# Token weights transposed by DMA between gated loads, column-tile transposes for q and k, and half of a batch prepared one stage later

## The chip, the cores and the metric

The kernel runs on one core of one Trainium2 chip. The metric is the device time of one execution in microseconds (us), as a median of several runs; lower is better. A profiled execution also gives a trace: when each instruction began and ended, what it waited for, when each DMA landed, and the share of the TensorE clock that was granted. The span in a trace (first to last instruction) is about 2 us shorter than the device time (in the profiled run of the kernel before 172.6 us against 174.73). PE is TensorE, DVE is VectorE, ACT is ScalarE, POOL is GpSimd, SP is SyncE. In this kernel GpSimd does almost nothing but issue the loads, which change fp32 to bf16 on the way (the "software queue", q0 in the profile). SyncE issues the transposes by DMA and the stores (the "hardware queue", q1).

## The reference, cut to what matters

```python
def _attn_ref(q, k, v, n_global, n_local):      # q, k, v: (4, 8, 768, 64)
    scores = scale * np.matmul(q, k.transpose(0, 1, 3, 2))
    # a window of 96 tokens, 8 global tokens, a bias that falls with the distance
    ...
    a = np.exp(scores - np.max(scores, axis=-1, keepdims=True))
    a = a / (np.sum(a, axis=-1, keepdims=True) + 1e-09)
    return np.matmul(a, v)

def _moe_ref(x, w_theta, w_tok_r, w_tok_i, w_ch):   # x: (4, 768, 512)
    theta = x @ w_theta
    zr, zi = x * np.cos(theta), x * np.sin(theta)
    y = np.einsum('ts,bsd->btd', w_tok_r, zr) + np.einsum('ts,bsd->btd', w_tok_i, zi)
    u = x + y
    return u + np.maximum(u @ w_ch, 0.0)
```

Attention gives x; then three stages follow for each batch: theta, the mixing over tokens with the two 768x768 token weights, and the channel product. The kernel overlaps the mixing of batch b with the attention of batch b+1. "The first mixing" is the stage in which batch 0 is mixed and batch 1's attention is computed.

## The kernel before

The loads are issued at the start, in one order, by GpSimd. The token weights come in by rows and are transposed, because the mixing as it is written takes them as its stationary operand (lhsT) with the source token on the partitions. PE transposes them into PSUM and DVE copies them out:

```python
def load_w():
    nc.gpsimd.dma_start(out=w_theta_bf, in_=...)
    for tt in range(0, NT, 2):
        for wi, src in enumerate((moe_w_tok_r, moe_w_tok_i)):
            w2 = moe.tile([T, 2, S], BF, name="w_nat", bufs=6)
            nc.gpsimd.dma_start(out=w2, in_=src[tt * T:(tt + 2) * T, :].rearrange(...))
            w_nat[wi, tt], w_nat[wi, tt + 1] = w2[:, 0], w2[:, 1]
    nc.gpsimd.dma_start(out=w_ch_bf, in_=...)

def trans_w(tt, copy=nc.vector.tensor_copy):
    for wi in range(2):
        ps = ps_small([T, NT, T], BF)
        for st in range(NT):
            nc.tensor.transpose(ps[:, st, :], w_nat[wi, tt][:, st * T:(st + 1) * T], ident)
        (copy if wi else nc.vector.tensor_copy)(out=w_tokT[wi][:, :, tt * T:(tt + 1) * T], in_=ps)
...
load_w()
load_all_qk(1)      # batch 1's q and k
load_all_v(1)       # batch 1's v
load_all_qk(2)
```

For batches 1 and 2, q and k of a pair of heads are put side by side by DVE (qkn), transposed by PE, and copied out by DVE (qT) and ACT (kT):

```python
def prep_copy(b, p):
    ...
    for i_ in range(2):
        nc.vector.tensor_copy(out=qkn[:, :, i_].rearrange("p t h d -> p h t d"),
                              in_=qk[:, i_, 2 * p:2 * p + 2])
def prep(b, p):
    ...
    for i_, dst in ((0, qT), (1, kT)):
        for t_ in range(NT):
            nc.tensor.transpose(ps[:, t_, :], qkn[:, t_, i_].rearrange("p h d -> p (h d)"), ident)
        # then qT copied by DVE, kT by ACT, and kG (DVE) made from kT
```

DVE makes a copy of batch 1's v (vG) before nearly all of batch 1's score products in its instruction order. And x of batches 1 to 3 is transposed by DMA (xT) before theta:

```python
def xtrans(b, p, ...):
    anchor["sp"] = nc.sync.dma_start_transpose(out=xT_sb[b][:, p, :]..., in_=x_sb[b][:, p]...)
```

The softmax here doesn't subtract the row's maximum and nothing guards it: scores larger than these inputs give would overflow.

Of the kernel before, what the change touches and what calls it, by code (L numbers as in the profile page):

```python
# [10 lines left out]
BF = mybir.dt.bfloat16  # L11
# [5 lines left out]
def kernel(  # L17
# [13 lines left out]
    nc = tc.nc  # L31
    B, H, S, D = q.shape
    T = 128
# [22 lines left out]
    def ps_small(shape, dtype):  # L56
        return small.tile(shape, dtype, name="ps", tag="ps")
# [90 lines left out]

    w_theta_bf = const.tile([T, NC, DM], BF)
    w_ch_bf = const.tile([T, NC, DM], BF)  # L150
    w_nat = {}
    w_tokT = [const.tile([T, NT, S], BF, name=f"w_tokT_{wi}") for wi in range(2)]

    def load_w():
        nc.gpsimd.dma_start(out=w_theta_bf, in_=moe_w_theta.rearrange("(c p) n -> p c n", p=T))
        for tt in range(0, NT, 2):
            for wi, src in enumerate((moe_w_tok_r, moe_w_tok_i)):
                w2 = moe.tile([T, 2, S], BF, name="w_nat", bufs=6)
                nc.gpsimd.dma_start(
                    out=w2, in_=src[tt * T:(tt + 2) * T, :].rearrange("(a p) s -> p a s", p=T))  # L160
                w_nat[wi, tt], w_nat[wi, tt + 1] = w2[:, 0], w2[:, 1]
        nc.gpsimd.dma_start(out=w_ch_bf, in_=moe_w_ch.rearrange("(c p) n -> p c n", p=T))

    def trans_w(tt, copy=nc.vector.tensor_copy):
        for wi in range(2):
            ps = ps_small([T, NT, T], BF)
            for st in range(NT):
                nc.tensor.transpose(ps[:, st, :], w_nat[wi, tt][:, st * T:(st + 1) * T], ident)
            (copy if wi else nc.vector.tensor_copy)(out=w_tokT[wi][:, :, tt * T:(tt + 1) * T], in_=ps)


    def warm(n):
        ps = ps_small([T, 512], FP)
# [13 lines left out]
    def behind(eng):  # L187

        return tc.issue_after(anchor[eng]) if eng in anchor else nullcontext()
# [29 lines left out]
                out=kG, in_=kT[:, T:(NT - 1) * T].rearrange("p (t n) -> p t n", t=NT - 2))  # L219
            nc.vector.tensor_copy(out=kG[:, :, 0:NG], in_=kT[:, None, 0:NG].to_broadcast([T, NT - 2, NG]))  # L220

    qkns = {}

    def prep_copy(b, p):
        qk = loads[b][0]
        qkn = qkns[b, p] = att.tile([T, NT, 2, 2, D], BF, name="qkn", bufs=2)
        with behind("dve"):
            for i_ in range(2):
                nc.vector.tensor_copy(  # L229
                    out=qkn[:, :, i_].rearrange("p t h d -> p h t d"), in_=qk[:, i_, 2 * p:2 * p + 2])  # L230

    def prep(b, p):
        if p == 0:
            prep_copy(b, 0)
        if p + 1 < NP:
            prep_copy(b, p + 1)
        qkn = qkns[b, p]
        qT = att.tile([T, S], BF, name="qT", bufs=6)
        kT = att.tile([T, S], BF, name="kT", bufs=6)
        for i_, dst in ((0, qT), (1, kT)):  # L240
            ps = ps_small([T, NT, T], BF)
            with behind("pe"):
                for t_ in range(NT):
                    nc.tensor.transpose(ps[:, t_, :], qkn[:, t_, i_].rearrange("p h d -> p (h d)"), ident)  # L244

            dst = dst.rearrange("p (n t) -> p n t", t=NT)
            src = ps.rearrange("p t n -> p n t")
            if i_ == 0:
                nc.vector.tensor_copy(out=dst, in_=src)
            else:  # L250
                nc.scalar.copy(out=dst, in_=src)

        qkT[(b, p)] = [qT, kT, None]
        kglob(b, p)

    def prep_dma(b, p):
        qk = loads[b][0]
        qkT[(b, p)] = [None, None, None]
        for i_ in (1, 0):
            to = qkT[(b, p)][i_] = att.tile([T, S], BF, name=("qT", "kT")[i_], bufs=6)  # L260
            with behind("sp"):
                nc.sync.dma_start_transpose(
                    out=to.rearrange("p (t s) -> p t s", t=NT),
                    in_=qk[:, i_, 2 * p:2 * p + 2].rearrange("p h t d -> p (h t d)"))
# [138 lines left out]
    def mix(b, tt, g):  # L403
        if g == 0:
            pss["mix"] = ps_small([T, DM], FP)
        ps = pss["mix"]
        for st in (2 * g, 2 * g + 1):
            for wi in range(2):
                anchor["pe"] = nc.tensor.matmul(  # L409
                    ps, lhsT=w_tokT[wi][:, st, tt * T:(tt + 1) * T], rhs=zri[b][:, wi, st, :],  # L410
                    start=(st == 0 and wi == 0), stop=(st == NT - 1 and wi == 1)).ins
        if g == NT // 2 - 1:
            u_sb[b, tt] = moe.tile([T, DM], BF, name="u", bufs=6)
            anchor["dve"] = nc.vector.tensor_add(  # L414
                u_sb[b, tt].rearrange("p (g d) -> p g d", g=NP), x_sb[b][:, :, tt, :],
                ps.rearrange("p (g d) -> p g d", g=NP)).ins
# [28 lines left out]
    def load_all_qk(b):  # L445
        alloc_qk(b)
        load_qk(b, 0, 8)

    def load_all_v(b):
        alloc_v(b)  # L450
        load_v(b, 0, 8)


    gate = const.tile([1, 1], BF)

    def load_behind(b, tile):
        g = nc.gpsimd.tensor_copy(out=gate, in_=tile).ins
        with tc.issue_after(g):
# [3 lines left out]
    def attention_steps(b, preps):  # L462

        steps = []
        add = lambda w, f, *a: steps.append((w, lambda: f(*a)))
        add(0, alloc_x, b)
        chunks = [(p, c) for p in range(NP) for c in range(NT // 2)]
        ahead = [preps[:1], preps[1:2], preps[2:]] if preps else [[]] * 3
        if b == B - 1:
            add(0, kglob, b, 0)  # L470
        for i_ in range(0, len(chunks), 2):
            steps.append((1800, lambda i_=i_: [scores(b, *pc) for pc in chunks[i_:i_ + 2]]))
            if i_ == 0:
                add(0, vglob, b, 0, H)
            if b == B - 1 and i_ in (0, 2, 6):
                add(0, kglob, b, (1, 2, 0, 3)[i_ // 2])
            if i_ == 8:
                steps.extend((1536, f) for f in ahead[0])
            for p in [p for p in range(NP) if (i_ // 2, p) in ((2, 0), (3, 1), (5, 2))]:
                add(1600, lambda p=p: [values(b, p, 0), values(b, p, 1)])  # L480
                add(800, xtrans, b, p)
        steps.extend((1536, f) for f in ahead[1])
        add(1600, lambda: [values(b, NP - 1, 0), values(b, NP - 1, 1)])
        add(800, xtrans, b, NP - 1)
        steps.extend((1536, f) for f in ahead[2])
        return steps
# [14 lines left out]
            side[i_][1]()  # L501
            i_ += 1

    load_w()
    load_all_qk(1)
    load_all_v(1)
    load_all_qk(2)
    alloc_x(0)
# [56 lines left out]
            xtrans(0, p - 1, act if p == NP - 1 else dve)  # L565
    values(0, NP - 1, 0)
    values(0, NP - 1, 1)
    trans_w(0, nc.scalar.copy)
    xtrans(0, NP - 1)
    for c in range(NT // 2):  # L570
        theta(0, c, 0)
# [8 lines left out]
    for b in range(B):  # L580
        nxt = b + 1 if b + 1 < B else None
        lag = 3
        th = [lambda c=c, j=j: theta(b, c, j) for c in range(NT // 2) for j in range(2)]
        pre = [lambda p=p: prep(1, p) for p in range(NP)] if b == 0 else []
        ahead = [[lambda p=p: prep(2, p) for p in range(NP)], [lambda p=p: prep_dma(3, p) for p in range(1)],
                 [], []][b]
        order = th[:4] + rest[:2] + th[4:] + rest[2:] if b else []
        if b == 2:
            order[:0] = [lambda p=p: prep_dma(3, p) for p in range(1, NP)]
        if b == 1:  # L590
            order.insert(0, lambda: load_behind(3, xT_sb[1][0:1, NC - 1, 0:1]))
        for f in order:
            f()
        main = []
        for tt in range(NT):
            for g in range(NT // 2):
                if (b, tt) != (B - 1, NT - 1):
                    main.append((2048, lambda tt=tt, g=g: mix(b, tt, g)))
                if b == 0 and g == 1 and tt + 1 < NT:
                    main.append((1536, lambda tt=tt: trans_w(tt + 1)))  # L600
                if tt >= lag and g == 0 and (b, tt) != (B - 1, NT - 1):
                    main.append((2048, lambda tt=tt: chan(b, tt - lag)))
                if b == 0 and tt and g == 1:
                    main.append((512, lambda tt=tt: utrans(b, tt - 1)))
            if b and (b, tt) != (B - 1, NT - 1):
                main.append((0, lambda tt=tt: utrans(b, tt)))
        side = [(1536, f) for f in pre]
        if b == 0:
            side[:0] = [(0, lambda: load_all_v(2))]
            side.append((0, lambda: (alloc_qk(3), load_qk_tokens(3, 0, H // 2))))  # L610
        side += attention_steps(nxt, ahead) if nxt else []
        weave(main, side, 0.3 if b == 0 else 0.0, 0.9)
        rest = [lambda tt=tt, b=b: chan(b, tt) for tt in range(NT - lag, NT)]
        if b == 0:
            rest.insert(1, lambda b=b: utrans(b, NT - 1))
# [44 lines left out]
```

## Time and profile before

| | before |
|---|---|
| median of 3 runs | 175.32 us (175.06 to 175.37) |
| span in the profile | 172.6 us |
| PE, DVE, ACT busy | 159.9, 128.5, 99.1 us |
| mean granted clock | 0.996 |

The page of the profile: first the busy time of each engine, then the span in 40 slices of 4.3 us, each digit the busy share of a slice in tenths.

```profile
PE 159.9 (93%) x1482; PEld 83.5 (48%) x1482; DVE 128.5 (74%) x288; ACT 99.1 (57%) x124; POOL 37.9 (22%) x45
...
PE   6479979999999999999999998999999989999991
...
DVE  7678965678999999999587588597786837724443
...
PEclk9999999999999999999999999999999999999998
DMA  5999999999999999879999997787138571323335
```

PE looks full from the seventh slice on. The row DMA is full too, from the second slice to the sixteenth: the loads run without a gap for 65 us. Windows of 5 us say the same in numbers. The last column is what the DMA moved in GB/s, counted in the bf16 that it writes; the DMA share before it is not used here:

```profile
core 0: us, PE busy (x) PEld busy (x) DVE busy (x) ACT busy (x) POOL busy (x), PEclk, DMA share, GB/s
20.00:25.00 5.00, 4.16 (x64) 2.17 (x62) 4.22 (x12) 3.26 (x4) 2.44 (x3) 1.00 1.16 209
30.00:35.00 5.00, 5.00 (x24) 2.18 (x23) 3.38 (x9) 5.00 (x7) 0.00 (x0) 1.00 1.28 205
...
45.00:50.00 5.00, 4.83 (x61) 3.18 (x59) 5.00 (x13) 3.24 (x5) 3.28 (x5) 1.00 1.72 190
50.00:55.00 5.00, 4.96 (x73) 2.88 (x71) 5.00 (x11) 3.93 (x5) 1.64 (x2) 1.00 1.67 189
```

From 45 to 60 us DVE is busy all the time, and the chain of work that ended last runs over it (start in us, length in us, what):

```profile
44.27 0.86 DVE qT L249
...
49.62 0.49 DVE kG L218
50.11 0.59 DVE e L312
50.81 0.59 DVE vG L333
51.40 0.60 DVE e L315
```

vG starts at 50.7 us here (the chain counts it from 50.81, when the instruction before it had ended). The v that it reads landed at 48.0 us, so DVE did not wait for it, but the slack is only 2.7 us.

### The profile page before, as it was taken

To read this page: it belongs to the slowest core of one execution; us is meant where nothing else is said; L and a number is where in the kernel's file an instruction comes from. 1 tells how busy PE (TensorE), PEld (TensorE's weight loads), DVE (VectorE), ACT (ScalarE), POOL (GpSimd) and SP (SyncE) were. 2 spreads that over 40 slices of the span, in tenths; PEclk is the share of its full clock that TensorE was granted. 3 is DMA by queue.
4 is the path that set the end of the run, shared out by engine and by line. 5 is a ranking of instruction groups with operands and counts; after the bars stand their busy time and mean duration, and the time that the engine had idled before them with its cause. 6 is when DMAs were issued, how large, how long until landed. Compare 5 with 4: busy or idle time off the path is not lost.

```text
span 172.6 us, 3652 instructions
## 1 busy us (share of the span) xinstructions
PE 159.9 (93%) x1482; PEld 83.5 (48%) x1482; DVE 128.5 (74%) x288; ACT 99.1 (57%) x124; POOL 37.9 (22%) x45
## 2 busy tenths in 40 slices
PE   6479979999999999999999998999999989999991
PEld 1245655455756566544455463444554634444440
DVE  7678965678999999999587588597786837724443
ACT  2479676999497595489834740979348308500010
POOL 8974355005272010099300000000000000000000
PEclk9999999999999999999999999999999999999998
DMA  5999999999999999879999997787138571323335
GB/s 146 192 193 178 210 208 209 204 204 171 160 204 175 166 155 128 132 97 154 210 141 80 224 158 165 138 152 226 30 76 113 135 171 40 142 41 102 100 93 182
DMA packets 75088, 25.92 MB, mean 150 GB/s; under 512 B 63168, under 2 KB 72128, under 8 KB 75072
## 3 DMA queue, kind: packets, MB, share of 16 engines
q0 software_dynamic: 45680, 12.45, 78.4%
q1 hardware_dynamic: 28976, 12.72, 36.6%
q10 hardware_dynamic: 416, 0.52, 0.9%
q8 instruction: 11, 0.18, 0.4%
q14 instruction: 5, 0.04, 0.1%
HBM read 25.69 MB, written 6.29 MB: 185 GB/s over the span
## 4 chain that ended last, share of the span: by engine, by line
PE 59%; DVE 21%; ACT 10%; DMA 6%; issue 1%; SPq 0%; DVEq 0%; ACTq 0%
PE ps L409 29%; PE ps L434 10%; PE pb L389 5%; PE pb L295 4%; PE pb L352 4%; DVE x_sb L362 4%; ACT etab L142 3%; PE ps L389 3%; ACT e L302 3%; DMA qk<-in_k_dram 3%; DVE kG L218 2%; DVE e L312 2%; ACT cs L395 2%; DMA kT<-qk 2%; DMA xT<-x_sb 2%; PE ps L244 2%
## 5 line engine op out<-in xcount | busy, mean ns | idle before, releaser
L409 PE MATMUL ps<-zri,w_tokT 128*128 128x512 bf16 x288 | 70.6, 380 | 0.3 <-DVE o_sb L440 0.2
L302 ACT ACTIVATE e<-pb 128x1024 bf16<-128x1024 f32 (+1 forms) x48 | 43.6, 958 | 23.1 <-PE pb L295 22.9
L409 PEld LDWEIGHTS <-w_tokT 128*128 128x128 bf16 x288 | 26.1, 98 | 29.0 <-issue 1.0
L414 DVE TENSOR_TENSOR u<-x_sb,ps 128x512 bf16<-128x512 bf16 x24 | 16.4, 682 | 14.6 <-PE ps L409 14.6
L434 PE MATMUL ps<-w_ch_bf,uT 128*128 128x512 bf16 x96 | 24.2, 379 | 0.0
L398 DVE TENSOR_TENSOR zri<-x_sb,cs 128x512 bf16<-128x512 bf16 x48 | 17.9, 418 | 8.0 <-ACT cs L395 7.8
L440 DVE SCALAR_TENSOR_TENSOR o_sb<-ps,u 128x512 f32<-128x512 f32 (+1 forms) x25 | 16.5, 662 | 3.1 <-PE ps L434 3.1
L395 ACT ACTIVATE cs<-pb,halfpi 128x1024 bf16<-128x1024 f32 x8 | 8.9, 1116 | 15.7 <-PE pb L389 15.7
L312 DVE TENSOR_TENSOR e<-e,etab 128x1024 bf16<-128x1024 bf16 (+1 forms) x24 | 14.7, 615 | 3.4 <-ACT e L302 3.4
L389 PE MATMUL pb<-w_theta_bf,xT 128*128 128x512 bf16 x64 | 15.2, 379 | 1.0 <-DMA xT<-x_sb 1.0
L295 PE MATMUL pb<-qT,kT 64*128 64x128 bf16 x224 | 15.6, 219 | 0.6 <-DVE qT L211 0.3
L295 PEld LDWEIGHTS <-kT 64*128 64x128 bf16 x224 | 9.0, 94 | 14.1 <-issue 12.5
L389 PEld LDWEIGHTS <-xT 128*128 128x128 bf16 x96 | 9.0, 98 | 12.0 <-DMA xT<-x_sb 2.4
L428 ACT COPY uT<-ps 128x512 bf16<-128x512 bf16 x7 | 4.1, 587 | 18.6 <-PE ps L427 18.6
L352 PEld LDWEIGHTS <-e 128*128 128x128 bf16 x352 | 12.7, 97 | 3.3 <-issue 1.5
L434 PEld LDWEIGHTS <-uT 128*128 128x128 bf16 x96 | 8.9, 98 | 10.0 <-ACT uT L428 0.3
L295 PE MATMUL pb<-qT,kG 64*128 64x128 bf16 x128 | 11.7, 217 | 1.2 <-DVE kG L220 1.2
L88 POOL DMA_DIRECT2D vn<-in_v_dram x5 | 9.7, 1930 | 12.2 <-DVE vn L68 10.6
L362 DVE TENSOR_TENSOR x_sb<-pb,rec 128x768 bf16<-128x768 f32 x12 | 11.4, 949 | 0.3
L315 DVE TENSOR_TENSOR e<-e,etab 128x1024 bf16<-128x1024 bf16 x12 | 8.2, 684 | 2.8 <-ACT e L302 2.8
L352 PE MATMUL pb<-vn,e 128*128 128x65 bf16 x168 | 9.6, 193 | 0.3 <-DVE x_sb L362 0.3
L82 POOL DMA_DIRECT2D qk<-in_q_dram x8 | 7.4, 920 | 8.8 <-DVE qkn L229 5.0
(74 smaller groups left out, 203.0 us busy)
## 6 DMA issues: line engine op xcount, KB each, us to landing
out_dram<-o_sb SPq DMA_DIRECT2D x23, 256.0 KB, 2.4
vn<-in_v_dram POOLq DMA_DIRECT2D x3, 768.0 KB, 22.7
qk<-in_q_dram POOLq DMA_DIRECT2D x2, 768.0 KB, 21.0
qk<-in_k_dram POOLq DMA_DIRECT2D x2, 768.0 KB, 23.6
w_nat<-in_moe_w_tok_r_dram POOLq DMA_DIRECT2D x3, 384.0 KB, 13.7
w_nat<-in_moe_w_tok_i_dram POOLq DMA_DIRECT2D x3, 384.0 KB, 14.6
vn<-in_v_dram POOLq DMA_DIRECT2D x2, 384.0 KB, 8.9
qk<-in_q_dram POOLq DMA_DIRECT2D x8, 96.0 KB, 9.7
```

Source lines behind the costliest of these rows:

```text
L295: nc.tensor.matmul(pb[:, hh, o:o + T], lhsT=lhsT, rhs=qT[R, (own, nxt)[part]], start=bool(b), stop=bool(b) or (jt == NT - 1 or (j == 1 and ...
L302: ins = nc.scalar.activation(e_c, pb[:, :, 0:n], AF.Exp, scale=scale).ins
L312: nc.vector.tensor_mul(e_c, e_c, tab[:, :, s0:s0 + n // T].rearrange("p a s n -> p a (s n)"))
L352: nc.tensor.matmul(o, lhsT=l_, rhs=r_, start=(i_ == 0), stop=(i_ == len(mms) - 1))
L362: nc.vector.tensor_mul(xv, po4[:, :, :, 0:D], rec.to_broadcast([T, n, NT, D]))
L389: nc.tensor.matmul(pb[j_] if last else pb[:, j_, :], lhsT=xT[:, dc, st(j_)], rhs=w_theta_bf[:, dc, :], start=(dc == 0), stop=(dc == NC - 1))
L395: nc.scalar.activation(o, p_, AF.Sin, **bias)
L398: nc.vector.tensor_mul(zri[b][:, i_, 2 * c + j_, :].rearrange("p (g d) -> p g d", g=NP), xb[:, :, 2 * c + j_, :], cs[:, i_, j_].rearrange( ...
L409: anchor["pe"] = nc.tensor.matmul(ps, lhsT=w_tokT[wi][:, st, tt * T:(tt + 1) * T], rhs=zri[b][:, wi, st, :], start=(st == 0 and wi == 0), ...
L414: anchor["dve"] = nc.vector.tensor_add(u_sb[b, tt].rearrange("p (g d) -> p g d", g=NP), x_sb[b][:, :, tt, :], ps.rearrange("p (g d) -> p g ...
L434: nc.tensor.matmul(ps_c, lhsT=uT[:, dc, :], rhs=w_ch_bf[:, dc, :], start=(dc == 0), stop=(dc == NC - 1))
L440: nc.vector.scalar_tensor_tensor(o_sb[:, cols], in0=ps_c[:, cols], scalar=0.0, in1=u[:, cols], op0=ALU.max, op1=ALU.add)
```

## The change

Its intent is to take work from PE and DVE in the first mixing. The token weights are transposed by DMA, from SyncE, so that PE and DVE have nothing to do with them. Such a transpose is slow beside the loads (in the trace before, an xT of 192 KB took 8.7 us to land beside the software queue and 2.7 alone), so the loads are gated: GpSimd waits until a pair of weights has landed before it issues the next loads. q and k are transposed without the copy qkn: each head's 64 columns are transposed by themselves into one half of the PSUM partitions, so that two transposes share the array as column tiles. And half of batch 2's preparation moves from the first mixing to the second.

```diff
-    w_tokT = [const.tile([T, NT, S], BF, name=f"w_tokT_{wi}") for wi in range(2)]
-    def load_w(): ...
-    def trans_w(tt, copy=nc.vector.tensor_copy): ...
+    w_tokT = [const.tile([T, NT, NT, T], BF, name=f"w_tokT_{wi}") for wi in range(2)]
+    gate = const.tile([1, 1], BF)
+    def after_load(tile):
+        return nc.gpsimd.tensor_copy(out=gate, in_=tile[0:1, 0, 0:1]).ins
+    def load_w_tok(tt):
+        for wi, src in enumerate((moe_w_tok_r, moe_w_tok_i)):
+            w2 = moe.tile([T, 2, S], BF, name="w_nat", bufs=6)
+            nc.gpsimd.dma_start(out=w2, in_=src[tt * T:(tt + 2) * T, :].rearrange(...))
+            nc.sync.dma_start_transpose(
+                out=w_tokT[wi][:, tt:tt + 2].rearrange("p a s t -> p (a s) t"),
+                in_=w2.rearrange("p a s -> p (a s)"))
+        return w2
...
-    def prep_copy(b, p): ...                      # the qkn copies
                 for t_ in range(NT):
-                    nc.tensor.transpose(ps[:, t_, :], qkn[:, t_, i_].rearrange("p h d -> p (h d)"), ident)
+                    for hh in range(2):
+                        nc.tensor.transpose(ps[hh * D:(hh + 1) * D, t_, :], qk[:, i_, 2 * p + hh, t_, :], ident)
...
+        late = [lambda p=p: prep(2, p) for p in range(NP // 2, NP)] if b == 2 else []
+            if i_ in (0, 2):
+                steps.extend((1536, f) for f in late[i_ // 2:i_ // 2 + 1])
...
-    load_w()
+    nc.gpsimd.dma_start(out=w_theta_bf, in_=...)
+    after_load(load_w_tok(0))
+    after_load(load_w_tok(2))
     load_all_qk(1)
+    after_load(load_w_tok(4))
+    nc.gpsimd.dma_start(out=w_ch_bf, in_=...)
     load_all_v(1)
     load_all_qk(2)
...
-        ahead = [[lambda p=p: prep(2, p) for p in range(NP)], ...
+        ahead = [[lambda p=p: prep(2, p) for p in range(NP // 2)], ...
-                if b == 0 and g == 1 and tt + 1 < NT:
-                    main.append((1536, lambda tt=tt: trans_w(tt + 1)))
```

More of the change, by code (lines that the diff above doesn't have):

```diff
@@ L150 @@
     w_ch_bf = const.tile([T, NC, DM], BF)
-    w_nat = {}
-    w_tokT = [const.tile([T, NT, S], BF, name=f"w_tokT_{wi}") for wi in range(2)]
-    def load_w():
-        nc.gpsimd.dma_start(out=w_theta_bf, in_=moe_w_theta.rearrange("(c p) n -> p c n", p=T))
-        for tt in range(0, NT, 2):
-            for wi, src in enumerate((moe_w_tok_r, moe_w_tok_i)):
-                w2 = moe.tile([T, 2, S], BF, name="w_nat", bufs=6)
-                nc.gpsimd.dma_start(
-                    out=w2, in_=src[tt * T:(tt + 2) * T, :].rearrange("(a p) s -> p a s", p=T))
-                w_nat[wi, tt], w_nat[wi, tt + 1] = w2[:, 0], w2[:, 1]
-        nc.gpsimd.dma_start(out=w_ch_bf, in_=moe_w_ch.rearrange("(c p) n -> p c n", p=T))
-    def trans_w(tt, copy=nc.vector.tensor_copy):
-        for wi in range(2):
-            ps = ps_small([T, NT, T], BF)
-            for st in range(NT):
-                nc.tensor.transpose(ps[:, st, :], w_nat[wi, tt][:, st * T:(st + 1) * T], ident)
-            (copy if wi else nc.vector.tensor_copy)(out=w_tokT[wi][:, :, tt * T:(tt + 1) * T], in_=ps)
+    w_tokT = [const.tile([T, NT, NT, T], BF, name=f"w_tokT_{wi}") for wi in range(2)]
[5 more added lines that the diff above has]
+            w2 = moe.tile([T, 2, S], BF, name="w_nat", bufs=6)
+            nc.gpsimd.dma_start(
+                out=w2, in_=src[tt * T:(tt + 2) * T, :].rearrange("(a p) s -> p a s", p=T))
+            nc.sync.dma_start_transpose(
+                out=w_tokT[wi][:, tt:tt + 2].rearrange("p a s t -> p (a s) t"),
+                in_=w2.rearrange("p a s -> p (a s)"))
+        return w2
     def warm(n):
@@ L220, in kglob, with prep @@
             nc.vector.tensor_copy(out=kG[:, :, 0:NG], in_=kT[:, None, 0:NG].to_broadcast([T, NT - 2, NG]))
-    qkns = {}
-    def prep_copy(b, p):
+    def prep(b, p):
         qk = loads[b][0]
-        qkn = qkns[b, p] = att.tile([T, NT, 2, 2, D], BF, name="qkn", bufs=2)
-        with behind("dve"):
-            for i_ in range(2):
-                nc.vector.tensor_copy(
-                    out=qkn[:, :, i_].rearrange("p t h d -> p h t d"), in_=qk[:, i_, 2 * p:2 * p + 2])
-    def prep(b, p):
-        if p == 0:
-            prep_copy(b, 0)
-        if p + 1 < NP:
-            prep_copy(b, p + 1)
-        qkn = qkns[b, p]
         qT = att.tile([T, S], BF, name="qT", bufs=6)
@@ L409, in mix @@
                 anchor["pe"] = nc.tensor.matmul(
-                    ps, lhsT=w_tokT[wi][:, st, tt * T:(tt + 1) * T], rhs=zri[b][:, wi, st, :],
+                    ps, lhsT=w_tokT[wi][:, tt, st, :], rhs=zri[b][:, wi, st, :],
                     start=(st == 0 and wi == 0), stop=(st == NT - 1 and wi == 1)).ins
@@ L451, in load_all_v @@
         load_v(b, 0, 8)
-    gate = const.tile([1, 1], BF)
     def load_behind(b, tile):
@@ L502, in weave @@
             i_ += 1
-    load_w()
+    nc.gpsimd.dma_start(out=w_theta_bf, in_=moe_w_theta.rearrange("(c p) n -> p c n", p=T))
+    after_load(load_w_tok(0))
+    after_load(load_w_tok(2))
     load_all_qk(1)
+    after_load(load_w_tok(4))
+    nc.gpsimd.dma_start(out=w_ch_bf, in_=moe_w_ch.rearrange("(c p) n -> p c n", p=T))
     load_all_v(1)
@@ L567 @@
     values(0, NP - 1, 1)
-    trans_w(0, nc.scalar.copy)
     xtrans(0, NP - 1)
@@ L584 @@
         pre = [lambda p=p: prep(1, p) for p in range(NP)] if b == 0 else []
-        ahead = [[lambda p=p: prep(2, p) for p in range(NP)], [lambda p=p: prep_dma(3, p) for p in range(1)],
+        ahead = [[lambda p=p: prep(2, p) for p in range(NP // 2)], [lambda p=p: prep_dma(3, p) for p in range(1)],
                  [], []][b]
```

## The prediction

> **What bounds the kernel now.** The page: PE 159.9 of 172.6 us busy (93%), clock 0.996. From the start-to-start steps of the matmuls (216 ns for 512 columns, 56 for 128, 30 for 65) PE is short of full rate by under 0.8 us in each 5 us after 28 us, except 45 to 60 us (1.2 to 1.6 each). There DVE is busy 5.00 of 5 us (windows view) and the chain of waits runs over DVE, from 44 to 61 us, then over PE. The DMA is a second limit, hidden: until 40 us the software queue writes 0.51 MB of bf16 per 2.5 us without a gap. Landings: batch 1's k 41.3 us, used at 41.3; its v 48.1, used at 50.7; batch 2's k 55.3, used at 59.2.
>
> **Removed.** 72 PE transposes of token weights (56 ns each, 4.0 us); the first 24 only fill waits for xT and zri, so 2.7 us count. DVE: eleven w_tokT copies (0.47 us, 5 us in all) and sixteen qkn copies (about 0.28, 4.5 us), nearly all at 36 to 71 us. That should end most of PE's waits for DVE, 2 us.
>
> **Added on PE.** 96 transposes more, of half width. The row-tiled pairs of the scores start 4 and 52 ns apart, so I expect a pair of column tiles to take the 56 ns of one full transpose. [...] the score groups lose 95 ns at entry and at exit. Nine groups: 1.7 us. If pairs don't overlap, 5 us more.
>
> **Moved.** Half of batch 2's preparation (two qT copies 0.87, kG 0.3 each) goes to the second mixing, where DVE has room.
>
> **Added on the DMA.** Six transposes of 384 KB. A 192 KB transpose lands in 2.7 us alone, but 8.7 beside a full software queue. The gates empty that queue: GpSimd issues nothing until a pair has landed. After the gate already present the first packet ended 2.2 us after the issue; with 0.5 us from last packet to landing and 0.25 for the gate, each of three gates leaves a hole of 3 us in a queue that had none. The transposes (0.2 to 0.24 MB per us) fit partly in the holes and take about 1 us each time from the loads behind. Estimated landings: batch 1's k 43 us, w_ch 53 (33.5 now; first used at 49.9), batch 1's v 58 to 60, batch 2's k 66.
>
> **Critical path.** The order of instructions puts the copy of batch 1's v into vG before all score products on DVE. After it DVE has 16 us of work until batch 1's last x_sb, which then is ready at about 76 us instead of 70.3; its transpose then meets batch 2's and 3's loads. So batch 1's theta starts about 5 us late, the savings already eaten. The rest is PE-bound and unchanged (+0.5 us).
>
> **Prediction: 179 us**, 8 in 10 between 172.5 and 185. Faster by over 2%: 0.17; within 2%: 0.26; slower by over 2%: 0.57.
>
> **What would show it.** Right: GpSimd waiting at three gate copies; v of batch 1 landing after 56 us; vG waiting for it by several us; PE idle at 50 to 62 us; column pairs 4 and 52 ns apart. Wrong: vG starting before 53 us; column transposes at 56 ns each.
>
> **What would make it wrong.** A shorter restart of the software queue, or transposes that hide wholly in the holes, would bring v back to 53 us and let the 4 to 5 us saved on PE and DVE through: about 172.

The 1.7 us for nine groups are 95 ns at entry and 95 ns at exit of each, as read from the score groups in the trace before (steps of about 312 instead of 216 ns and of 151 instead of 55).

## The result, and the profile after

The changed kernel takes 198.55 us in the median of 4 runs (196.35 to 201.37; one of them, 201.37, slow). The kernel before took 175.34 us beside it. The ratio is 1.1275 (95% interval 1.1172 to 1.1379). A ratio is the mean time of one kernel's fast runs over that of the other's in the same rounds, so it is not quite the ratio of the medians. Executions over 1.5% slower than the fastest of the same kernel are left out of the means. Slower was right; the size, 3.7 us predicted and 23 us measured, was not.

The same lines of the page:

```profile
PE 161.6 (82%) x1481; PEld 81.0 (41%) x1506; DVE 123.0 (62%) x261; ACT 98.5 (50%) x123; POOL 37.9 (19%) x48
...
PE   5589869921986269994899999979999998999991
...
DVE  6779846501373397883387887858687782843342
...
PEclk9999999975589957999799999999999999999998
DMA  5999988999999999999799938877934456132434
```

The loss lies between the eighth slice and the nineteenth (slices of 4.9 us, so 35 to 95 us). PE and DVE are idle there in turns, and the granted clock falls to half. Counted from the steps between starts of matmuls, PE falls 23.1 us short of its full rate between 35 and 70 us (5.9 before), and 9.3 us between 70 and 95 us (1.7 before). The difference of the two sums, 24.8 us, is about that of the spans, 24.5 us. It is no exact account: 25 of the changed kernel's 1506 matmuls left no record, which counts about 5 us too much over the whole span; outside this stretch PE falls 8.6 us further short than before; and about 4 us of work on PE are gone.

The windows show it from two sides. The DMA moves less than before in the stretches around the gates (124 instead of 209 GB/s at 20 us, 145 instead of 205 at 30) although the transposes are counted in it, and at 45 us the engines wait while it moves no less than before (208 and 190):

```profile
core 0: us, PE busy (x) PEld busy (x) DVE busy (x) ACT busy (x) POOL busy (x), PEclk, DMA share, GB/s
20.00:25.00 5.00, 4.03 (x66) 2.23 (x64) 4.15 (x12) 3.50 (x4) 0.00 (x0) 1.00 1.00 124
30.00:35.00 5.00, 4.63 (x23) 1.90 (x22) 3.58 (x10) 5.00 (x7) 0.00 (x0) 1.00 0.86 145
...
45.00:50.00 5.00, 1.65 (x25) 1.24 (x26) 0.96 (x1) 0.00 (x0) 0.00 (x0) 0.50 1.25 208
50.00:55.00 5.00, 4.67 (x35) 2.16 (x35) 1.54 (x3) 1.35 (x2) 1.63 (x3) 0.50 0.92 166
```

The chain that ended last is now a chain of loads and gates. Each load's length here runs from its issue to its landing:

```profile
11.71 13.94 DMA w_nat<-in_moe_w_tok_i_dram
25.72 0.18 POOL gate L156
25.95 0.71 POOL w_nat L161
26.66 8.63 DMA w_nat<-in_moe_w_tok_i_dram
35.42 0.33 POOL gate L156
35.87 1.78 POOL qk L73 x2
37.65 0.68 POOL w_nat L161
38.32 14.63 DMA w_nat<-in_moe_w_tok_i_dram
...
54.32 13.13 DMA vn<-in_v_dram
67.47 0.71 DVE vG L316
...
88.11 6.12 DMA xT<-x_sb
```

So vG starts at 67.5 us instead of 50.7, the moment batch 1's v lands. And the waits (engine, line, waited for, total us, times, longest):

```profile
POOL gate L156 <- DMA w_nat<-in_moe_w_tok_i_dram: 35.3, 3, 14.0
DVE vG L316 <- DMA vn<-in_v_dram: 6.8, 1, 6.8
...
PE ps L392 <- DMA w_tokT<-w_nat: 3.2, 2, 2.8
```

Before, neither of the last two waits existed. The column tiles did what was predicted: in the trace their pairs start 3 to 4 ns apart and the next pair 52 to 53 ns later in most of the groups at the whole clock. In parts of two groups, soon after the clock had come back at 55.4 us, it is 0 to 1 and 55 ns, or all transposes follow evenly after 25 to 31 ns; a pair takes 55 to 57 ns there too.

The whole can be read from a few moments. This table has them for every kernel, from the completion records of the traces (us from the start of the span): when batch 1's k and v landed, when batch 1's last x_sb was given to the DMA for its transpose, when that xT landed, and the end.

| kernel | k1 | v1 | last x_sb | xT landed | end |
|---|---|---|---|---|---|
| before | 41.3 | 48.0 | 70.4 | 73.5 | 172.6 |
| after | 49.2 | 67.5 | 88.1 | 94.2 | 197.1 |
| e1 column tiles alone | 41.3 | 48.5 | 68.9 | 72.7 | 173.0 |
| e2 e1, half of batch 2 later | 42.0 | 48.3 | 69.2 | 72.0 | 173.1 |
| e3 e2 with the gates | 44.3 | 61.9 | 82.4 | 85.2 | 186.7 |
| e4 after without the gates | 39.6 | 62.3 | 83.2 | 90.4 | 192.7 |
| e5 before with v later | 42.1 | 56.1 | 76.1 | 78.9 | 178.4 |
| e6 e2, no weight transposes | 41.5 | 47.7 | 68.1 | 73.8 | 175.2 |
| e7 after with v earlier (slow) | 46.4 | 52.7 | 84.3 | 91.1 | 196.0 |
| e8 after with PE kept busy | 48.5 | 67.5 | 87.3 | 93.3 | 197.4 |
| e9 e6, a later load moved | 41.5 | 48.4 | 68.1 | 71.2 | 172.9 |
| e10 e1, the same load moved | 42.7 | 48.6 | 69.6 | 72.3 | 175.0 |
| e11 before, the same load moved (slow) | 42.6 | 48.6 | 70.9 | 73.6 | 180.2 |
| e12 before, no weight transposes | 41.8 | 48.1 | 68.5 | 72.2 | 173.0 |

The difference after minus before splits at these moments: v lands 19.4 us later; from v to xT it takes 1.3 us more; from xT to the end 3.8 us more. Together 24.5 us.

### The profile page after: what moved, and what is told of

Read it like the earlier page. It is cut to its first block, busy times and chain, and to the rows that moved or that the text cites. A ratio compares the mean times of both kernels' runs of the same rounds, so it can differ in the third digit from the quotient of the medians.

```text
span 197.1 us, 3660 instructions
## 1 busy us (share of the span) xinstructions
PE 161.6 (82%) x1481; PEld 81.0 (41%) x1506; DVE 123.0 (62%) x261; ACT 98.5 (50%) x123; POOL 37.9 (19%) x48
## 3 DMA queue, kind: packets, MB, share of 16 engines
q0 software_dynamic: 45680, 12.45, 67.5%
## 4 chain that ended last, share of the span: by engine, by line
PE 48%; DMA 36%; DVE 8%; POOL 3%; issue 2%; SPq 1%; DVEq 0%; POOLq 0%
PE ps L392 26%; DMA w_nat<-in_moe_w_tok_i_dram 19%; DMA vn<-in_v_dram 11%; PE ps L417 8%; DMA xT<-x_sb 5%; PE pb L278 5%; PE pb L335 4%; PE pb L372 2%; PE ps L372 2%; POOL qk L73 2%; DVE o_sb L423 2%; DMA kT<-qk 1%; PE ps L227 1%; DVE zri L381 1%; DVE x_sb L345 1%
## 5 line engine op out<-in xcount | busy, mean ns | idle before, releaser
L392 PE MATMUL ps<-zri,w_tokT 128*128 128x512 bf16 x273 | 71.8, 393 | 4.4 <-DMA w_tokT<-w_nat 3.2
L417 PE MATMUL ps<-w_ch_bf,uT 128*128 128x512 bf16 x92 | 23.3, 379 | 1.9 <-DMA w_ch_bf<-in_moe_w_ch_dram 1.7
L372 PE MATMUL pb<-w_theta_bf,xT 128*128 128x512 bf16 x61 | 16.3, 401 | 5.6 <-DMA xT<-x_sb 5.3
L335 PEld LDWEIGHTS <-e 128*128 128x128 bf16 x352 | 13.2, 99 | 9.7 <-DVE e L295 5.0
L372 PEld LDWEIGHTS <-xT 128*128 128x128 bf16 x96 | 9.1, 100 | 18.5 <-DMA xT<-x_sb 8.0
L232 DVE COPY qT<-ps 128x768 bf16<-128x768 bf16 x8 | 7.6, 951 | 14.0 <-PE ps L227 14.0
L335 PE MATMUL pb<-vn,e 128*128 128x65 bf16 x168 | 10.5, 197 | 5.9 <-DVE e L295 4.7
L227 PE MATMUL ps<-ident,qk 128*64 128x128 bf16 x192 | 8.8, 245 | 5.4 <-DMA qk<-in_k_dram 3.0
L234 ACT COPY kT<-ps 128x768 bf16<-128x768 bf16 x8 | 6.4, 799 | 13.1 <-PE ps L227 12.9
```

The lines of the kernel that those rows point to most:

```text
L227: nc.tensor.transpose(ps[hh * D:(hh + 1) * D, t_, :], qk[:, i_, 2 * p + hh, t_, :], ident)
L335: nc.tensor.matmul(o, lhsT=l_, rhs=r_, start=(i_ == 0), stop=(i_ == len(mms) - 1))
L372: nc.tensor.matmul(pb[j_] if last else pb[:, j_, :], lhsT=xT[:, dc, st(j_)], rhs=w_theta_bf[:, dc, :], start=(dc == 0), stop=(dc == NC - 1))
L392: anchor["pe"] = nc.tensor.matmul(ps, lhsT=w_tokT[wi][:, tt, st, :], rhs=zri[b][:, wi, st, :], start=(st == 0 and wi == 0), stop=(st == NT ...
L417: nc.tensor.matmul(ps_c, lhsT=uT[:, dc, :], rhs=w_ch_bf[:, dc, :], start=(dc == 0), stop=(dc == NC - 1))
```

## The experiments

My theory after the result: the loads before v are the chain, the gates leave holes in it and the transposes lengthen it. Rivals: the column tiles cost the time; the move of half of batch 2 does; the transposes alone do, whatever the gates; the lowered clock does.

### e1 and e2: the parts that touch no load

e1 is the kernel before with the new `prep` (column tiles, no qkn) and nothing else. e2 adds the later preparation of half of batch 2:

```diff
 # e1: prep as in the change; load_w, trans_w and the order of loads as before
 # e2: in addition
+        late = [lambda p=p: prep(2, p) for p in range(NP // 2, NP)] if b == 2 else []
+            if i_ in (0, 2):
+                steps.extend((1536, f) for f in late[i_ // 2:i_ // 2 + 1])
-        ahead = [[lambda p=p: prep(2, p) for p in range(NP)], ...
+        ahead = [[lambda p=p: prep(2, p) for p in range(NP // 2)], ...
```

> The kernel before with one part of the change: q and k of batches 1 and 2 transposed as pairs of column tiles, no qkn copies. Weights stay on PE, loads ungated, batch 2 prepared in the first mixing. My theory (the whole loss comes from the loads): 173 to 176 us, DVE 4 us less busy, pairs of starts 4 and 52 ns apart, PE at full clock. Rival (the column tiles cost the time[...]): over 185 us.

> As e1, with half of batch 2 prepared in the second mixing. Theory: within 1 us of e1. Rival (moving that work into the second mixing costs): 3 us or more over e1.

Measured: e1 175.22 us, ratio 1.0006 (0.9964 to 1.0048); e2 175.74 us, ratio 1.0024 (0.9983 to 1.0066). Both are the same as before, so neither part carries the loss. They bring no gain either. In e1, DVE is busy 125.3 us instead of 128.5, and the last x_sb is ready 1.5 us sooner. But from xT's landing to the end it takes 100.3 us where the kernel before takes 99.1. In the trace each excursion of PE into column tiles costs about 95 ns at entry and again at exit (steps of 309 instead of 216 ns and of 151 instead of 55). The weight loads of the column tiles took 109 ns in the mean, where those of the same transposes took 97 before, and the pairs still started every 55 to 57 ns. These excursions all lie before xT's landing, so they do not explain the longer stretch after it. In e2 that stretch is 101.1 us. The moved work may be paid there, but e12 below has a longer stretch too without any of it.

### e3 and e4: gates without transposes, transposes without gates

With e2 (neither) and the changed kernel (both) these two fill a square of four. e3 is e2 with the gates and the new order of loads, and the weights still transposed on PE. e4 is the changed kernel without the gates.

```diff
 # e3, on e2
-    load_w()
+    nc.gpsimd.dma_start(out=w_theta_bf, in_=...)
+    after_load(load_w_tok(0))     # loads only; trans_w on PE as before
+    after_load(load_w_tok(2))
     load_all_qk(1)
+    after_load(load_w_tok(4))
+    nc.gpsimd.dma_start(out=w_ch_bf, in_=...)
 # e4, on the changed kernel
-    after_load(load_w_tok(0))
+    load_w_tok(0)                 # and so for 2 and 4
```

> As e2, with the three gates and the load order of the changed kernel, but the weights still transposed on PE. It has the holes of the queue without the transposes. If the gate alone makes a hole of 3 us (as I predicted): batch 1's v lands at 57 to 58 us and the time is 179 to 183 us; then the rest of the 198.5 comes from the transposes standing in the holes. If the gates alone make holes of 5 to 6 us: v lands near 67 us and the time is 190 us or more.

> The changed kernel without the three gates: transposes by DMA beside a full software queue. Theory (the gates' holes carry most of the loss): batch 1's v lands before 60 us, 178 to 188 us, with PE waiting for w_tokT at 33 to 45 us because each transpose lands 8 us or more after its issue. Rival (the 2.36 MB of transposes cost the same wherever they stand): 195 us or more, v at 65 us or later.

Measured, medians of fast runs:

| | loads not gated | loads gated |
|---|---|---|
| weights transposed on PE | 175.74 (e2), v at 48.3 | 188.41 (e3), v at 61.9 |
| weights transposed by DMA | 195.28 (e4), v at 62.3 | 198.11 (after), v at 67.5 |

(The changed kernel ran in another round. The kernel before took 175.34 us beside it and 175.00 us beside the other three.) The gates alone cost 12.7 us, the transposes alone 19.5 us, both together 22.4 us. They are not a sum, since the transposes run largely in the holes: in the trace of the changed kernel 0.72 to 0.73 of a pair's 0.79 MB moved, at each gate, between the last packet of the load before and the first of the load behind. Both of my expectations were missed. e3 was slower than 179 to 183 us, with v at 61.9 us, between the two values that I had set against each other. e4's time, 195.28 us, is what I had written for the rival (195 or more), but its v, at 62.3 us, is not (65 or later). Nor does the rival's account hold, that the transposes cost the same wherever they stand: they add 19.5 us without gates and 9.7 us with them.

The holes can be measured in the packets. I call a hole a stretch in which the software queue moved less than a quarter of its usual 0.2 MB per us (in steps of 0.25 us, each packet counted where it ends). Before 57 us the kernel before has none of 0.75 us or more. e3 has three of 4.25, 3.5 and 4.25 us, 12.0 in all. The changed kernel has 6.75, 5.5 and 4.75 us, 17.0 in all. e4 has two short ones before 57 us, 1.75 us in all, but its loads slow down beside the transposes: from 46 to 54 us they move 0.05 to 0.07 MB per us, just above that mark. With the mark at 60% of the usual rate the stretches that begin before 57 us add up to 13.25 us in e3, 19.25 in the changed kernel and 13.5 in e4 (none before), nearly what v is late in each against e2: 13.6, 19.2 and 14.0 us. So the rate that this one queue lost accounts for the late v in all three.

I had put the hole at 3 us because after the gate already in the kernel the first packet ended 2.2 us after the issue. In e3 the first packet ended 1.6 to 1.8 us after the issue, which is less, and from the last packet to the first it took only 2.2 to 2.7 us. But the full rate (here: three quarters of the usual one, over half a microsecond) came only 2.0 to 3.2 us after the issue, and the last packets before the gate trickle in too. In the changed kernel, where transposes stand in the hole, the first packet took 2.8 to 3.1 us and the full rate 3.6 to 4.3. At the first gate the last data packet ended at 23.7 us and the load was reported landed only at 25.66, while a transpose was under way (in e3: 23.8 and 24.1). At the other two gates the report came 0.3 us after the last packet.

The chain of e3 shows the gates without any transpose:

```profile
25.10 6.48 DMA w_nat<-in_moe_w_tok_i_dram
31.71 0.23 POOL gate L157
...
34.61 13.50 DMA w_nat<-in_moe_w_tok_i_dram
...
49.48 12.42 DMA vn<-in_v_dram
61.93 0.71 DVE vG L333
```

In e4 the chain is the transposes themselves. SyncE needs 4 to 10 us to issue one, where it needed 1.4 to 1.7 in the changed kernel, and it issues them one after the other. They landed 10.4 to 20.6 us after their issue, against 3.8 to 8.0 in the changed kernel:

```profile
21.88 4.23 SPq L163
26.11 0.06 issue
26.17 8.41 SPq L163
34.62 9.71 SPq L163
44.38 11.07 DMA w_tokT<-w_nat
55.49 0.82 PE ps L392 x3
```

and PE waits for the weights:

```profile
PE ps L392 <- DMA w_tokT<-w_nat: 15.1, 3, 10.7
```

So the gates of the change do what they are meant to do (the waits for w_tokT fall from 15.1 to 3.2 us) and cost at least as much on the other side (198.11 us against 195.28).

### e5: the load of v made late, and nothing else

```diff
     load_all_qk(1)
-    load_all_v(1)
     load_all_qk(2)
+    load_all_v(1)
```

The order of instructions on PE, DVE, ACT and SyncE is the same as before; only GpSimd issues in another order.

> The kernel before with one thing changed: batch 2's q and k are loaded before batch 1's v. No gate, no transpose by DMA, no column tile. It makes batch 1's v late by about 7 us (55 instead of 48 us) and nothing else earlier in need. Theory (everything up to batch 1's theta hangs on that v, at 20 us from v to the last x_sb, as in the changed kernel): 4 to 6 us slower, 179 to 182 us. Rival (as I predicted: DVE needs only 16 to 17 us after v and catches up most of it): at most 2 us slower.

Measured: 180.78 us, ratio 1.0357 (1.0318 to 1.0396). v landed at 56.1 us instead of 48.0, DVE waited for it, and everything after it moved:

```profile
DVE vG L333 <- DMA vn<-in_v_dram: 5.2, 1, 5.2
```

8.1 us of delay give 6.0 us of time; the kernel before has 2.7 us of slack before vG. From vG's start to the last x_sb it takes 19.9 us here (56.1 to 76.1), 19.7 before (50.7 to 70.4), 20.6 after, 20.5 in e3. My prediction had 16 us of DVE work there. The windows between these moments have DVE busy 19.7 of 19.7 us before, 19.7 of 19.9 in e5, and 18.5 of 20.6 in the changed kernel. So after v nothing is caught up, which was the second thing that I had wrong: DVE itself had more to do than I had counted.

### e8: the lowered clock

PE stands idle for 5 us before batch 1's first values in the changed kernel, and its clock is at 0.50 when it resumes. e8 fills that wait with work that does nothing:

```diff
+                if (b, p) == (1, 0):
+                    add(0, warm, 20)      # 20 matmuls of zeros, 512 columns
                 add(1600, lambda p=p: [values(b, p, 0), values(b, p, 1)])
```

> The changed kernel with 20 idle matmuls of 512 columns put on PE just before batch 1's first values, where PE waited 5 us for v. They keep PE busy in the wait, so that the granted clock should not fall to 0.5 at 70 us. If the lowered clock adds to the loss: 2 to 3 us faster than the changed kernel, 195 to 196.5 us. If not: 198 us or slightly more.

Measured: 199.09 us (198.46 to 199.44), not faster than the fast runs of the changed kernel (198.11). The clock was indeed kept up. First the changed kernel, then e8, the same window:

```profile
70.00:75.00 5.00, 4.09 (x34) 1.82 (x32) 4.74 (x9) 0.70 (x1) 1.16 (x2) 0.50 1.53 214
```

```profile
70.00:75.00 5.00, 3.69 (x51) 2.06 (x50) 4.97 (x10) 1.92 (x3) 1.17 (x2) 1.00 1.59 210
```

Both are bound by DVE in that window (4.74 and 4.97 of 5 us). The last x_sb came 0.8 us sooner, and the end did not. So the fall of the clock at this wait costs up to 0.8 us as far as x_sb, and nothing of that reaches the end. The falls at 40 to 55 us and at 90 to 95 us were not tested.

### e7: v loaded earlier in the changed kernel

```diff
     load_all_qk(1)
+    load_all_v(1)
     after_load(load_w_tok(4))
     nc.gpsimd.dma_start(out=w_ch_bf, in_=...)
-    load_all_v(1)
     load_all_qk(2)
```

> The changed kernel with batch 1's v loaded before the last pair of token weights instead of after it and w_ch. Theory (v is the last wait of the chain): v lands at 56 to 58 us instead of 67.5, then the last pair's transposes (landing at 67 us or later) become the wait; 190 to 196 us. If v were not the wait: no change, 198 us.

Measured: 198.05 us in the median of 4 runs, but three of them, the profiled one too, were slow, and the one fast run took 194.59 us. That falls inside what I expected, but one run gives no verdict. The trace shows where the wait went: v lands at 52.7 us, vG starts at 55.1, and from 57.1 us DVE stands still until the first channel product, whose weights w_ch now land last, at 63.6 us. The line is DVE's first o_sb, with the idle time before it and what ended it:

```profile
65.61 0.69 DVE L423 SCALAR_TENSOR_TENSOR o_sb<-ps,u 128x512 f32<-128x512 f32 x1 [8.49 <-PE ps L417]
```

This reordering, the only one that I tried, made another load come too late. The same amount of data has to pass before the first mixing can end.

### e6, e9 and e12: what the change could have gained at best

These three give a wrong result: the token weights are loaded straight into the tile that the mixing reads and are never transposed. The products of the mixing are as many and as large as before, the numbers in them are other numbers. The edit, shown against the changed kernel's loads:

```diff
-            w2 = moe.tile([T, 2, S], BF, name="w_nat", bufs=6)
-            nc.gpsimd.dma_start(out=w2, in_=src[...])
-            nc.sync.dma_start_transpose(out=w_tokT[wi][...], in_=w2...)
+            nc.gpsimd.dma_start(out=w_tokT[wi][:, tt:tt + 2].rearrange("p a s t -> p a (s t)"), in_=src[...])
```

e6 has this on top of e2. e12 has it on top of the kernel before, without column tiles. e9 is e6 with batch 3's first loads of q and k moved behind the gate that waits for batch 1's last xT:

```diff
-            side.append((0, lambda: (alloc_qk(3), load_qk_tokens(3, 0, H // 2))))
-            load_qk_tokens(b, H // 2, H // 2)
+            alloc_qk(b)
+            load_qk_tokens(b, 0, H)
```

> Wrong result on purpose: as e2 (column tiles, half of batch 2 late, loads in the old order without gates), with the token weights loaded straight into the tile that the mixing reads, never transposed. It shows what the change could have gained if the transposes cost nothing at all. My prediction's credit (2.7 us of PE work, 2 us of waits for DVE): 170 to 172 us. Rival (the removed work was off the critical path): 174 us or more.

> Wrong result on purpose: as e6 (weights never transposed), with batch 3's first loads of q and k moved behind the gate that already waits for batch 1's last xT. e6 gained nothing; in its trace the last xT took 5.7 us to land beside the software queue, and PE stood idle for 3.9 us in it. If that wait ate the gain: xT lands in about 3 us and the time falls to 173 to 174.5 us. If not: 176.5 us or more.

> Wrong result on purpose: the kernel before with nothing changed but that the token weights are loaded straight into the tile that the mixing reads, and their 72 PE transposes and 12 copies are left out. q and k are prepared as before, no column tiles, nothing late. It is the most that moving these transposes off PE could have brought. My prediction credited 2.7 us of PE work and part of 2 us of waits: 171 to 173 us. Rival (the first mixing is bound by when its loads land, as e6 and e9 suggest): 174 to 176 us.

Measured: e6 177.10 us, ratio 1.0137 (1.0109 to 1.0164), a little slower than before, though within the 2% that count as the same. e9 175.31 us, ratio 1.0013 (0.9982 to 1.0044). e12 175.22 us, ratio 0.9996 (0.9952 to 1.0039). Even when the transposes of the weights cost nothing at all, the kernel was not faster. In e6 the last xT meets the loads of the software queue. The piece of the chain, in e6 and then in e9:

```profile
68.11 5.72 DMA xT<-x_sb
```

```profile
68.11 3.08 DMA xT<-x_sb
```

That wait explains 1.8 us of e6, as e9 shows, though less than I expected of e9 (173 to 174.5 us). e12 has the last x_sb ready 1.9 us sooner than before; xT lands 1.3 us sooner; and the stretch after it is 100.8 us instead of 99.1. What is saved in the first mixing is given back in the second. In e12's profiled execution it can be seen where: the second mixing ends with an xT of batch 2 that took 4.6 us to land, with PE waiting. It was issued 1.3 us sooner than before (103.25 against 104.58 us) and landed 0.5 us later (107.8 against 107.3). PE waited 2.3 us for it, 0.5 before.

```profile
103.25 4.57 DMA xT<-x_sb
```

Why that transfer was slow, and why in the other kernels too the later stages take up every microsecond saved before them, is not settled. For the first mixing itself the traces name a limit: in e9 the chain begins with the landing of batch 1's k (41.5 us), and vG starts as v lands (48.4 us), so faster engines then meet the loads.

### e10 and e11: a try at a faster kernel

Both have the same edit of batch 3's loads as e9, on e1 and on the kernel before.

> A try at a better kernel: e1 (column tiles, weights on PE, no gates) with the same loads of batch 3 moved behind the gate. In e1 the last xT took 3.8 us to land. If that wait was on the chain: 174 us, about 1 us better than e1 and before. If PE had other work in it: 175 us, the same.

> The kernel before with only those loads moved behind the gate. The last xT took 3.1 us to land before, and PE was busy meanwhile: the same, 174.5 to 175.5 us. Slower (177 or more) if batch 3's q and k, about 8 us later, then come too late for the transposes of the second mixing.

Measured: e10 176.95 us, ratio 1.0101 (1.0077 to 1.0125), slower than both values that I had written; e11 180.79 us in the median, ratio 1.0285 (1.0230 to 1.0340). The tries failed. e11 did what its expectation named as the danger: batch 3's first transposes by DMA are late. One takes 8.6 us to land (2.8 in the median before), beside the load of batch 3's v as I read it, which no run tested; an xT of batch 2, behind them in the chain, is issued at 109.49 us (from the trace of e11, which was slow):

```profile
98.70 8.55 DMA kT<-qk
```

No version that I ran beats the kernel before.

## Why the prediction was wrong

The direction and the chain (gates, a late v, a late last x_sb) were right, the size was not: 179 us predicted, 198.55 measured, outside the range. The steps that failed are the landing of v (holes and transposes both taken too small: 67.5 us, not 58 to 60), the work of DVE after it, and the credit for the work removed. One by one:

- **What bounds the kernel.** "The DMA is a second limit, hidden" was right, and stronger than I said. e12 shows that the work on the weights was worth 1.3 us at batch 1's last xT and nothing at the end.
- **"Removed ... 2.7 us count" and "2 us" of waits for DVE.** Wrong. e12 leaves all of the weights' work out and gains nothing (175.22 against 175.00 us); e1 leaves the qkn copies out and gains nothing. The last x_sb is 1.5 to 1.9 us sooner in these kernels, and what follows it is longer by at least as much.
- **"Nine groups: 1.7 us", and pairs in 56 ns.** Right in kind: pairs 3 to 4 and 52 to 53 ns apart, about 95 ns at entry and exit, e1 neutral.
- **"Each of three gates leaves a hole of 3 us".** Mis-sized. Without transposes the holes were 4.25, 3.5 and 4.25 us (e3), with them 6.75, 5.5 and 4.75 (after). I took the first packet for the return of the stream. From last to first packet e3's gaps are 2.2 to 2.7 us, even less than my 3; but the full rate came up to 1.5 us after the first packet. With transposes in the hole the first packet came 1.1 to 1.5 us later than in e3, and at the first gate the report of the load before it 1.7 us later.
- **The transposes "take about 1 us each time from the loads behind".** Mis-sized. Comparing e3 with the changed kernel they put v off by 5.6 us (61.9 to 67.5). Without gates they put it off by 14.0 us (48.3 to 62.3, e2 and e4).
- **v at "58 to 60" us.** It was 67.5.
- **"After it DVE has 16 us of work", so the late v costs only 5 us.** Mis-sized. In the changed kernel the stretch took 20.6 us, and DVE was busy for 18.5 of them: 2.5 us more work than I had counted, and 2.1 us of waiting. In e8, with the clock kept up, it took 19.8 us, with DVE busy for the same 18.5. The other kernels take 19.6 to 20.5 us there, except e12 (18.6) and e7 (29.2, where w_ch was waited for). e5 shows the effect alone: v 8.1 us late, 6.0 us lost.
- **"The rest is PE-bound and unchanged (+0.5 us)".** After xT the changed kernel takes 102.9 us, before 99.1. 2.0 of the 3.8 us are in e2 too, but e12, without column tiles and moved preparation, is 1.7 us longer there as well. So what the 3.8 us belong to stays open.

With the measured sizes the sum comes out: v 19.4 us later, less the slack of 2.7 us before vG, is 16.7 us; 0.9 us more from vG to x_sb; xT 3.0 us slower to land (6.1 instead of 3.1 us, beside the loads that are late as well); 3.8 us after it: 24.4 us, against 24.5 in the spans. These terms are read from the same two traces, so they have to add up. That a late v by itself costs most of its delay is what e5 shows; the last two terms, 6.8 us, were not tested by themselves.

## What to carry to other kernels

Before moving work from an engine to the DMA, look at when the loads land and when they are first used: batch 1's k was used here the moment it landed (41.3 us), and full engines (PE 93% busy) hid this second limit. Here transposes by DMA put the load of v off by 5.6 us between gates and by 14.0 us without them. A gate in the full queue cost here the time from the last packets at full rate before it to the first at full rate after it (4.25 to 4.5 us each in e3 at the 60% mark), not the 2.2 to 2.7 us from last packet to first; measure that stretch in packets. And to learn what a saving is worth, leave the work out altogether and time the wrong result (e12): it took one experiment, and run first it would have ended the idea at the start.
